# Reordering the first two units' chains of a fused recurrence and expert-mixture kernel

## The chip, the cores and the metric

The kernel runs on one core of a Trainium2 chip. The time is the device time of one execution in microseconds (us). Engines are named as the profile names them: PE is the matrix engine (PEld its weight loads), DVE the vector engine, ACT the scalar engine, POOL the GpSimd engine, and SP the engine that issues nearly all DMA transfers. Each engine works through its own instructions in order and waits on semaphores for the others.

## The reference

The first half is a linear recurrence over 768 time steps for 4 batches and 8 heads with head dimension 40. The second half takes its output as 3072 tokens of 320 numbers and runs four dense two-layer experts over every token, mixed by normalized probabilities.

```
for t in range(S):                      # r,k,v,w,a,b: (4, 8, 768, 40)
    y[:, :, t] = einsum('bhd,bhde->bhe', rt, state)
    Sa = einsum('bhde,bhe->bhd', state, at)
    state = state * wt[:, :, None, :] - einsum('bhd,bhe->bhde', Sa, bt)
    state = state + einsum('bhd,bhe->bhde', vt, kt)
x = y.transpose(0, 2, 1, 3).reshape(3072, 320)
p = domain_probs / (domain_probs.sum(-1, keepdims=True) + 1e-9)
for e in range(4):                      # w1: (4, 320, 1024), w2: (4, 1024, 320)
    out += p[:, e:e+1] * (maximum(x @ w1[e], 0) @ w2[e])
```

## The kernel before

The sequence is cut into 12 chunks of 64 steps, and the batches into two pairs. One pair of batches in one chunk is a *unit*: 24 units, numbered 0 to 23, with units 0 and 1 holding the first chunk. Everything is float32.

For each unit `within(q)`, a generator that the main code advances piece by piece with `run(gen, n)`, computes what needs no state. It transposes the decays `rawW` into `G` and runs a scan for their running products (L413 to L423). PE transposes `G` into `pg`; DVE forms `gp = 1 / (pg * W)` and with it the scaled inputs `n_tok` and `k_tok`, and scales the transposed `AT` by `G`. PE transposes `n_tok` and `k_tok` (`pNT`, `pKT`, copied by ACT into `NT`, `KT`), and multiplies the score matrices `pfe` (which ACT copies to `F`, and DVE masks into `ET`), `pev` (which gives `EV`), and `pc` (the scores of `V` and `R`, masked by DVE into `VC`). For the first three units `V` and `R` are transposed on PE (`pVT`, `pRT`, in `turn_rv`); later units do it on DVE.

`substitute(q, eng)` solves unit-triangular 32x32 systems: it copies `blocks` from `F`, transposes them into `M`, and goes through 16 double columns of `Z`. The first two units do it on DVE, with one product and one reduction for each double column; later units do it on POOL while DVE does other work. `merge(q)` turns the solved `Z` into `Qc` and `QTc`, joins the 32-blocks into 64-blocks on PE (`pY`, `pQ`, both copied by ACT) and fills `QT`. `step(q)` then carries the state: `psat` and `pst`, copies on ACT, `pxr` masked by DVE into `SX`, `pdy` (the output `Y` and the new state, on DVE), and `pxT`, which places `Y` as columns of `xT` for the experts.

The experts follow as pieces of work in a list, taken out by `mix(n)`. In `mixture_of_unit`, used for units 0 and 1, `ups(e)` multiplies `xT` by two pieces of `w1` into `ph` and ACT writes `relu` to `hs`; `down(e)` multiplies `hs` by `w2` into `po`, which DVE scales by the gate and adds to `osb`. `normalize()` forms the gates from the probabilities (`pp` on PE, five small DVE operations). `ph` and `po` share three buffers of PSUM, tagged `mm`; all the other products share five, tagged `big`. Later chunks use a saving scheme of seven products in place of eight.

The order of work around the change is written out by hand, after the definition of `keep_warm`. `keep_warm(n)` issues n products of the identity with itself, whose result nobody reads; each shows as two matrix instructions in the profile. Calls of `load`, `load_raw`, `load_piece` and `load_w2` stand in the same order and go to SP's queue one behind the other. A load into a buffer waits in that queue until the buffer's last reader is done, and all behind it wait too: `rawW` and `rawA` have one buffer each, the `w1` pieces two plus three that borrow `sums`. `tc.keep_in_program_order` (`pin`) fixes an instruction's place on its engine; otherwise a scheduler chooses. From unit 1 on a loop over the units takes over.

Of the kernel before, what the change touches and what calls it, by code (L numbers as in the profile page):

```python
# [15 lines left out]
def kernel(  # L16
# [42 lines left out]
    P = 128  # L59
# [284 lines left out]
    def by(x, n):  # L344
        return x.rearrange("p (h e) -> p h e", e=n)
# [56 lines left out]
    def within(q):  # L402
# [11 lines left out]
        for i in range(2):  # L414
# [1 line left out]
        q.gl = sb.tile([P, 2 * NJ, 1], FP32, name="gl", tag="gl", bufs=4)  # L416
        pin(nc.vector.tensor_tensor(out=q.gl[:], in0=G[:, L::L][:, :, None], in1=first[:, :, 0:1], op=ALU.mult))
        pin(nc.vector.memset(Gv[:, :, 0:1], 0.0))
        pin(nc.vector.tensor_tensor_scan(
            out=G[:, 0:2 * NJ * L], data0=G[:, 0:2 * NJ * L],  # L420
            data1=first[:].rearrange("p c i -> p (c i)"), initial=0.0, op0=ALU.mult, op1=ALU.add,
        ))
        nc.vector.tensor_tensor(out=q.gl[:], in0=q.gl[:], in1=Gv[:, :, L - 1:L], op=ALU.mult)  # L423
        q.AT = sb.tile([P, 2 * NJ, L], FP32, name="AT", tag="AT", bufs=2)
        if q.u == 0:
            pin(turn_raw(q.AT[:], n["rawA"][:]))
        yield

        pg = by(turn("pg", tok(Gv), q.u == 2)[:], 64)[:, :, 0:D]
        gp = sb.tile([P, H, D], FP32, name="gp")  # L430
        pin(nc.vector.tensor_tensor(out=gp[:], in0=pg, in1=n["W"][:], op=ALU.mult))
        pin(nc.vector.reciprocal(out=gp[:], in_=gp[:]))  # L432

        def turn_rv():
            VT = sb.tile([P, 2 * NJ, L], FP32, name="VT", tag="turned", bufs=3)
# [10 lines left out]
            return VT  # L446

        if q.u == 1:
            VT = turn_rv()
        yield  # L450

        def turned(name, x):
# [16 lines left out]
            out=q.N[:, :, 0:D], in0=n["B"][:], scalar=-1.0, in1=gp[:], op0=ALU.mult, op1=ALU.mult,  # L469
        )  # L470
        pin(ins)
        pin(nc.vector.tensor_tensor(out=q.K[:, :, 0:D], in0=n["K"][:], in1=gp[:], op=ALU.mult))
        if q.u > 0:
            pin(turn_raw(q.AT[:], n["rawA"][:]))
        at_ij = q.AT[:].rearrange("p (i j) t -> p i j t", i=2)
        ins = nc.vector.tensor_tensor(out=at_ij, in0=at_ij, in1=Gv.rearrange("p (j i) t -> p i j t", i=2), op=ALU.mult)
        pin(ins)
        q.VC = VCs()
        if q.u > 0:
# [4 lines left out]

        NT = turned("NT", q.N)
        KT = turned("KT", q.K)
        yield

        if q.u > 0:
            if q.u == 2:  # L490
                VT = turn_rv()
            causal_scores(VT)
            yield

# [16 lines left out]
        ))  # L511
        if not q.apart:
            copy_F()
            yield

        ET = ETs()
# [16 lines left out]
            causal_scores(turn_rv())  # L533
        yield

    def substitute(q, eng, between=None):

        blocks = sb.tile([P, H, Q], FP32, name="blocks")
        for i in range(P // Q):
            move = nc.scalar.copy if i >= 2 else nc.vector.tensor_copy  # L540
            tc.keep_in_program_order(move(out=blocks[quarter(i)], in_=q.F[quarter(i), :, quarter(i % 2)]))  # L541
        q.below = belows()
        for i in (1, 3):
            tc.keep_in_program_order(nc.gpsimd.tensor_copy(out=q.below[quarter(i)], in_=q.F[quarter(i), :, 0:Q]))  # L544
# [12 lines left out]
        by_second = Z[:, 1:3].rearrange("p x k r -> p (x k) r")  # L557
        below = M[:].rearrange("p c r -> p (c r)")[:, 1::2 * (Q + 1)]
        ins = nc.vector.tensor_tensor(
            out=by_second, in0=pairs[:, :, 1, :], in1=below[:, :, None].to_broadcast([P, Q // 2, Q]), op=ALU.mult,  # L560
        )
        tc.keep_in_program_order(ins)
        ins = nc.vector.tensor_tensor(out=pairs[:, :, 0, :], in0=pairs[:, :, 0, :], in1=by_second, op=ALU.add)  # L563
        tc.keep_in_program_order(ins)
        run(between)
        at_once = eng is nc.vector
        for x in (0, 3) if at_once else (0,):
            tc.keep_in_program_order(eng.tensor_copy(out=Z[:, x], in_=unit_cols[:]))
        for j in range(0, Q, 2):
            n, m = j // 4 + 1, Q - 1 - j  # L570
            here = 3 * (j // 2 % 2) if at_once else 0
            ins = eng.tensor_tensor(  # L572
                out=Z[:, 1:3, 0:n, j + 1:Q], in0=M[:, j:j + 2, None, j + 1:Q].to_broadcast([P, 2, n, m]),
                in1=Z[:, here, 0:n, j:j + 2].rearrange("p k x -> p x k")[:, :, :, None].to_broadcast([P, 2, n, m]),
                op=ALU.mult,
            )
            if j == 0:
                tc.keep_in_program_order(ins)
            z = Z[:, :, 0:n, j + 1:Q]
            if at_once:  # L580
                terms = z[:, 0:3] if here == 0 else z[:, 1:4]
                eng.tensor_reduce(out=z[:, 3 - here], in_=terms.rearrange("p x k r -> p k r x"), op=ALU.add, axis=AX.X)
            else:
                for x in range(1, 3):
                    eng.tensor_tensor(out=z[:, 0], in0=z[:, 0], in1=z[:, x], op=ALU.add)  # L585
        if at_once:

            odd, even = (Z[:, x].rearrange("p k (r four) -> p k r four", four=4)[:, :, :, 1:3] for x in (3, 0))
            eng.tensor_copy(out=even, in_=odd)
# [405 lines left out]
    def keep_warm(n):  # L995

        for _ in range(n):
            ins = matmul(out=warm[:, 0:P], lhsT=ident[:], rhs=ident[:], start=True, stop=True)
            tc.keep_in_program_order(ins)

    ws = [within(units[u]) for u in range(3)]
    norm = normalize()
    keep_warm(16)
# [10 lines left out]
    go(load_raw(units[2], "W"))  # L1014
    load_probs()
    run(ws[0], 2)

    def scores_of_first():
        run(ws[0], 1)
        yield  # L1020

    substitute(units[0], nc.vector, scores_of_first())
    run(ws[0], 1)
    set_pick()
    m, s = merge(units[0]), begin_step(0)
    run(m, 1)
    run(ws[0])
    load(units[2], "W")
    for x in "VR":
        load_padded(units[2], x)  # L1030
    load_piece()
    load_piece()
    run(ws[1], 1)
    run(norm, 1)
    keep_warm(18)
    run(ws[1], 1)
    run(m)
    run(ws[2], 1)
    run(norm)
    load(units[2], "BK")  # L1040
    go(load_raw(units[2], "A"))
    go(load_raw(begin(3), "W"))
    load_w2(0)
    load_piece()
    load_piece()
    load_w2(1)
    load_piece()
    run(s, 2)
    run(ws[1], 1)
    run(s)  # L1050
    run(ws[1], 2)

    def scores_of_second():
        run(ws[1], 1)
        yield

    mixture_of_unit(units[0])
    substitute(units[1], nc.vector, scores_of_second())
    run(ws[1])
    mix(3)  # L1060
    m, s = merge(units[1]), begin_step(1)
    run(m, 1)
    mix(1)
    run(ws[2], 1)
    run(m)
    run(s, 2)
    run(ws[2], 1)
    load(units[3], "WBKV")
    go(load_raw(units[3], "AVR"))
    mix(1)  # L1070
    run(ws[2], 3)
    substitute(units[2], nc.gpsimd)
    run(ws[2], 1)
    ws.append(within(units[3]))
    run(ws[3], 1)
    mix(1)

    sparse = range(4 * 1, 4 * 4 + 2)

# [124 lines left out]
```

## Time and profile before

| | |
|---|---|
| median of 3 runs | 1113.57 us (1108.56 to 1113.94) |
| the profiled execution | 1112.43 us, its span 1110.2 us, mean granted PE clock 0.988 |
| busy: PE, PEld | 1075.2 us (97%), 959.7 us (86%) |
| busy: DVE, POOL, ACT | 758.1 us (68%), 501.5 us (45%), 352.9 us (32%) |
| moved by DMA | 122.18 MB, 110 GB/s on average |

Busy times are those of one profiled execution, counted from the start of its span. A timeline row gives the start, the busy time, the engine and line, the operation, what it writes and reads, how many instructions were joined in the row, and in brackets the idle time of the engine just before with what ended it. A row of the windows gives, for a stretch of time, its length, the busy time of PE, PEld, DVE, ACT and POOL (with counts), the PE clock granted (1.00 is full speed), the DMA engines' busy share and the GB/s moved. PE is busy for nearly all of the span, and its gaps lie in the first 160 us.

### The profile page before, as it was taken

How to read it: one execution, taken by the hardware profiler on the slowest of the kernel's cores; microseconds unless marked ns; L12 is line 12 of the kernel's file. 1: busy time of each engine (PE TensorE's matmuls, PEld its weight loads, DVE VectorE, ACT ScalarE, POOL GpSimd, SP SyncE). 2: the span in 40 equal slices, each digit the busy share in tenths (PEclk: the TensorE clock that was granted, in tenths of full speed). 3: DMA queues.
4: the chain of work that ended last, by engine and by line, in shares of the span. 5: the costliest groups of instructions: out<-in, count | busy, mean ns of one | idle time of the engine just before them, and what ended most of it. 6: DMA issues, size and time to landing. Idle time of an engine off the chain costs nothing.

```text
span 1110.2 us, 38530 instructions
## 1 busy us (share of the span) xinstructions
PE 1075.2 (97%) x16100; PEld 959.7 (86%) x16100; DVE 758.1 (68%) x1553; ACT 352.9 (32%) x956; POOL 501.5 (45%) x1272
## 2 busy tenths in 40 slices
PE   6799899999999999999999999999999999999998
PEld 5677788788898998989989899998989989988887
DVE  8765578888777767768667677767677677543443
ACT  2323434333333233232342333332432332322110
POOL 5004576781643734634635636536437346330000
PEclk8899999999999999999999999999999999999999
DMA  7785535444354364454443453543553532222320
GB/s 120 207 249 139 115 77 127 112 98 113 96 135 94 93 156 101 104 123 112 103 120 89 121 120 93 125 104 98 132 109 80 145 88 65 90 77 70 101 87 12
DMA packets 268868, 122.18 MB, mean 110 GB/s; under 512 B 213736, under 2 KB 242072, under 8 KB 268696
## 3 DMA queue, kind: packets, MB, share of 16 engines
q1 hardware_dynamic: 265416, 119.12, 43.6%
q8 instruction: 127, 2.08, 0.8%
q10 hardware_dynamic: 3280, 0.61, 0.3%
q14 instruction: 45, 0.37, 0.1%
HBM read 111.79 MB, written 3.93 MB: 104 GB/s over the span
## 4 chain that ended last, share of the span: by engine, by line
PE 77%; DVE 4%; POOL 3%; ACT 2%; issue 2%; SPq 2%; DMA 1%; DVEq 0%; POOLq 0%
PE ph L76 34%; PE p L76 27%; PE pdy L76 2%; POOL Z L585 2%; PE psat L76 2%; PE pxr L76 2%; PE prn L76 1%; PE po L76 1%; PE pfe L76 1%; POOL Z L572 1%; PE pQ L76 1%; PE pc L76 1%; PE pev L76 1%; PE pe L76 1%; PE pY L76 1%
## 5 line engine op out<-in xcount | busy, mean ns | idle before, releaser
L76 PE MATMUL ph<-xT,w1p 128*128 128x256 f32 (+3 forms) x3040 | 445.1, 376 | 1.9 <-issue 1.7
L76 PEld LDWEIGHTS ph<-xT,w1p 64*64 64x64 f32 (+1 forms) x3040 | 337.5, 161 | 70.2 <-issue 26.9
L585 POOL TENSOR_TENSOR Z<-Z 128x31 f32<-128x31 f32 (+7 forms) x704 | 256.7, 365 | 55.1
L889 DVE TENSOR_TENSOR a<-hs 128x512 f32<-128x512 f32 x220 | 151.3, 705 | 106.3 <-ACT hs L770 106.1
L572 POOL TENSOR_TENSOR Z<-M,Z 128x62 f32<-128x62 f32 (+7 forms) x352 | 148.5, 422 | 130.1 <-DVE M L563 104.2
L770 ACT ACTIVATE hs<-ph 128x512 f32<-128x512 f32 (+1 forms) x208 | 115.1, 564 | 229.0 <-PE ph L76 227.8
L76 PE MATMUL p<-sums,a 128*128 128x160 f32 x1056 | 164.9, 299 | 0.0
L76 PEld LDWEIGHTS p<-sums,a 128*128 128x128 f32 x1056 | 152.8, 190 | 2.2
L783 DVE SCALAR_TENSOR_TENSOR osb<-p,gate,osb 128x320 f32<-128x320 f32 (+1 forms) x243 | 108.1, 481 | 57.7 <-PE p L76 53.5
L544 POOL COPY below<-F 32x256 f32<-32x256 f32 x48 | 23.0, 480 | 219.8 <-ACT F L502 218.2
L76 PE MATMUL p<-w,a 128*128 128x160 f32 x704 | 106.2, 301 | 0.8 <-ACT hs L770 0.6
L76 PE MATMUL p<-w,hs 128*128 128x160 f32 x704 | 102.9, 299 | 0.0
L76 PEld LDWEIGHTS p<-w,hs 128*128 128x128 f32 x704 | 100.2, 190 | 2.2
L76 PEld LDWEIGHTS p<-w,a 128*128 128x128 f32 x704 | 98.3, 190 | 3.9 <-ACT hs L770 3.9
L604 POOL COPY QT<-QTc 32x256 f32<-32x256 f32 x96 | 50.2, 523 | 75.8 <-DVE QTc L598 38.6
L547 DVE STREAM_TRANSPOSE M<-blocks 128x1024 f32<-128x1024 f32 x24 | 47.3, 1972 | 38.3 <-ACT blocks L541 38.2
L692 ACT COPY RS<-pxr 64x256 f32<-64x256 f32 x88 | 32.3, 367 | 108.7 <-DVE SX L400 60.0
L432 DVE RECIPROCAL gp<-gp 128x320 f32<-128x320 f32 x24 | 51.6, 2151 | 0.7
L529 ACT COPY EV<-pev 64x160 f32<-64x160 f32 x96 | 23.1, 286 | 89.3 <-PE pev L76 89.0
L619 ACT COPY QT<-pQ 32x128 f32<-32x128 f32 x96 | 24.6, 257 | 59.4 <-PE pQ L76 57.7
L596 DVE STREAM_TRANSPOSE Qc<-Z 128x256 f32<-128x256 f32 x24 | 15.1, 628 | 39.9 <-POOL Z L585 39.8
L651 ACT COPY SN<-prn 128x256 f32<-128x256 f32 x44 | 14.9, 372 | 78.5 <-DVE RH L646 77.4
(147 smaller groups left out, 1369.2 us busy)
## 6 DMA issues: line engine op xcount, KB each, us to landing
w1p<-in_moe_w_dram SPq DMA_DIRECT2D x95, 512.0 KB
w1p<-in_moe_w_dram SPq DMA_DIRECT2D x190, 64.0 KB
w<-in_moe_w_dram SPq DMA_DIRECT2D x4, 1280.0 KB
sums<-in_moe_w_dram SPq DMA_DIRECT2D x9, 512.0 KB
natW<-in_w_dram SPq DMA_DIRECT2D x48, 80.0 KB
natB<-in_b_dram SPq DMA_DIRECT2D x48, 80.0 KB
natK<-in_k_dram SPq DMA_DIRECT2D x48, 80.0 KB
out_dram<-osb SPq DMA_DIRECT2D x46, 80.0 KB
```

Of the source, the lines that this page charges most:

```text
L76: return stated(nc.tensor.matmul(**k))
L432: pin(nc.vector.reciprocal(out=gp[:], in_=gp[:]))
L529: nc.scalar.copy(out=of_slot(q.EV[half(p)], i ^ p)[:, :, 0:D], in_=pev[i][half(p)])
L547: ins = nc.vector.transpose(out=M[:], in_=cols)
L572: ins = eng.tensor_tensor(out=Z[:, 1:3, 0:n, j + 1:Q], in0=M[:, j:j + 2, None, j + 1:Q].to_broadcast([P, 2, n, m]), in1=Z[:, here, 0:n, j: ...
L585: eng.tensor_tensor(out=z[:, 0], in0=z[:, 0], in1=z[:, x], op=ALU.add)
L604: ins = nc.gpsimd.tensor_copy(out=q.QT[quarter(i), :, quarter(i % 2)], in_=QTc[quarter(i)])
L619: nc.scalar.copy(out=of_slot(to[quarter(2 * r)], y), in_=src)
L692: nc.scalar.copy(out=RS[half(s), x ^ s::2], in_=prs[x][half(s)].rearrange("p (j i) t -> p j i t", i=2),)
L770: nc.scalar.activation(out=h[:, i * HF // 2:(i + 1) * HF // 2, 0:n], in_=ph[i][:], func=ACTF.Relu,)
L783: nc.vector.scalar_tensor_tensor(out=to, in0=p, scalar=sc, in1=to, op0=ALU.mult, op1=ALU.add)
L889: nc.vector.tensor_tensor(out=t[:], in0=x, in1=y, op=op)
```

## The change

The change is in the generator `within` and in the order written out by hand; no product of the computation is added or taken away.

- **Spare products.** The 18 directly ahead of the first merge go. 12 are put behind unit 0's `pe`, 4 behind its `pc`, 3 ahead of the merge.
- **Unit 1's chain.** Its scan moves behind unit 0's solve on DVE (the transposes of `G` stay ahead of it). `turn_rv` is called at a yield of its own. `pg` moves behind `pQ` of the merge, `pNT` and `pKT` behind `pdy`; its `k_tok` and its scaling of `AT` go from DVE to POOL.
- **Unit 1's solve** begins behind unit 0's `Y`. It has a new argument `during`, which issues other work between its columns: the gates of `normalize` and the first `down`.
- **Unit 2's chain.** `G` and its scan go behind unit 1's merge transposes on DVE; `V` and `R` are turned right behind `KT`; `pc` goes behind `pfe`, and `ET` ahead of `blocks`.
- **Loads.** On SP's queue `w2` of the first expert and the pieces behind it stand ahead of unit 2's `B` and `K`. Unit 3's `rawW` goes from ahead of all these to behind `w2` of the third expert, ahead of pieces 7 and 8. Pieces 9 and 10 of `w1` stand ahead of unit 3's `W`, `B`, `K`, `V`, `A` and `R`.
- **PE's order** is fixed to program order from the start and not only from the loop on.

From `pdy` of unit 1 on, the instructions of PE stand in the same order in both kernels.

```diff
@@ within(q)
         pin(nc.vector.memset(Gv[:, :, 0:1], 0.0))
-        pin(nc.vector.tensor_tensor_scan(...))
-        nc.vector.tensor_tensor(out=q.gl[:], in0=q.gl[:], in1=Gv[:, :, L - 1:L], op=ALU.mult)
         q.AT = sb.tile([P, 2 * NJ, L], FP32, name="AT", tag="AT", bufs=2)
-        if q.u == 0:
-            pin(turn_raw(q.AT[:], n["rawA"][:]))
-        yield
...
         if q.u == 1:
+            yield
             VT = turn_rv()
+            yield
+        pin(nc.vector.tensor_tensor_scan(
...
+        if q.u < 2:
+            pin(turn_raw(q.AT[:], n["rawA"][:]))
+        yield
+
+        pg = by(turn("pg", tok(Gv), q.u == 2)[:], 64)[:, :, 0:D]
...
-        pin(nc.vector.tensor_tensor(out=q.K[:, :, 0:D], in0=n["K"][:], in1=gp[:], op=ALU.mult))
-        if q.u > 0:
+        other = nc.gpsimd if q.u == 1 else nc.vector
+        pin(other.tensor_tensor(out=q.K[:, :, 0:D], in0=n["K"][:], in1=gp[:], op=ALU.mult))
+        if q.u > 1:
             pin(turn_raw(q.AT[:], n["rawA"][:]))
...
-        ins = nc.vector.tensor_tensor(out=at_ij, in0=at_ij, ...)
+        ins = other.tensor_tensor(out=at_ij, in0=at_ij, ...)
...
         KT = turned("KT", q.K)
-        yield
-
-        if q.u > 0:
-            if q.u == 2:
-                VT = turn_rv()
+        if q.u == 2:
+            VT = turn_rv()
+        yield
+
+        if q.u == 1 or q.u >= PADDED:
             causal_scores(VT)
             yield
...
         if not q.apart:
             copy_F()
+            if q.u == 2:
+                causal_scores(VT)
             yield
@@ substitute
-    def substitute(q, eng, between=None):
+    def substitute(q, eng, between=None, during=None):
...
         for j in range(0, Q, 2):
+            if during:
+                during(j)
@@ the order by hand
+    in_order[0] = True
     ws = [within(units[u]) for u in range(3)]
...
     load_probs()
     run(ws[0], 2)
-    def scores_of_first():
+    keep_warm(12)
+    def scores_of(u):
...
-    substitute(units[0], nc.vector, scores_of_first())
+    substitute(units[0], nc.vector, scores_of(0))
     run(ws[0], 1)
     set_pick()
     m, s = merge(units[0]), begin_step(0)
     run(m, 1)
     run(ws[0])
+    keep_warm(4)
+    run(norm, 1)
+    run(ws[1], 1)
+    keep_warm(3)
     load(units[2], "W")
     for x in "VR":
         load_padded(units[2], x)
     load_piece()
     load_piece()
     run(ws[1], 1)
-    run(norm, 1)
-    keep_warm(18)
-    run(ws[1], 1)
-    run(m)
-    run(ws[2], 1)
-    run(norm)
-    load(units[2], "BK")
     go(load_raw(units[2], "A"))
-    go(load_raw(begin(3), "W"))
     load_w2(0)
     load_piece()
     load_piece()
+    run(m)
+    run(ws[1], 1)
+    run(s, 3)
+    run(ws[1], 1)
+    run(s, 1)
+    run(ws[1], 1)
+    run(s)
+    load(units[2], "BK")
     load_w2(1)
     load_piece()
-    run(s, 2)
-    run(ws[1], 1)
-    run(s)
     run(ws[1], 2)
...
     mixture_of_unit(units[0])
-    substitute(units[1], nc.vector, scores_of_second())
-    run(ws[1])
-    mix(3)
+    def during_second(j):
+        if j in (0, 14):
+            mix(1)
+        if j == 4:
+            run(ws[1])
+        if j == 12:
+            run(norm)
+    substitute(units[1], nc.vector, scores_of(1), during_second)
     m, s = merge(units[1]), begin_step(1)
     run(m, 1)
+    run(ws[2], 1)
+    go(load_raw(begin(3), "W"))
+    mix(2)
+    run(ws[2], 1)
+    run(m, 1)
+    lead()
+    run(m)
     mix(1)
     run(ws[2], 1)
-    run(m)
     run(s, 2)
     run(ws[2], 1)
     load(units[3], "WBKV")
     go(load_raw(units[3], "AVR"))
+    run(ws[2], 2)
+    substitute(units[2], nc.gpsimd)
     mix(1)
-    run(ws[2], 3)
-    substitute(units[2], nc.gpsimd)
-    run(ws[2], 1)
     ws.append(within(units[3]))
     run(ws[3], 1)
-    mix(1)
```

More of the change, by code (lines that the diff above doesn't have):

```diff
@@ L418, in within @@
         pin(nc.vector.memset(Gv[:, :, 0:1], 0.0))
[L419 to L422, printed above, removed]
-        nc.vector.tensor_tensor(out=q.gl[:], in0=q.gl[:], in1=Gv[:, :, L - 1:L], op=ALU.mult)
-        q.AT = sb.tile([P, 2 * NJ, L], FP32, name="AT", tag="AT", bufs=2)
-        if q.u == 0:
-            pin(turn_raw(q.AT[:], n["rawA"][:]))
-        yield
[L429 to L432, printed above, removed]
+        q.AT = sb.tile([P, 2 * NJ, L], FP32, name="AT", tag="AT", bufs=2)
         def turn_rv():
@@ L448, in within @@
         if q.u == 1:
+            yield
             VT = turn_rv()
+            yield
+        pin(nc.vector.tensor_tensor_scan(
+            out=G[:, 0:2 * NJ * L], data0=G[:, 0:2 * NJ * L],
+            data1=first[:].rearrange("p c i -> p (c i)"), initial=0.0, op0=ALU.mult, op1=ALU.add,
+        ))
+        nc.vector.tensor_tensor(out=q.gl[:], in0=q.gl[:], in1=Gv[:, :, L - 1:L], op=ALU.mult)
+        if q.u < 2:
+            pin(turn_raw(q.AT[:], n["rawA"][:]))
+        yield
+        pg = by(turn("pg", tok(Gv), q.u == 2)[:], 64)[:, :, 0:D]
+        gp = sb.tile([P, H, D], FP32, name="gp")
+        pin(nc.vector.tensor_tensor(out=gp[:], in0=pg, in1=n["W"][:], op=ALU.mult))
+        pin(nc.vector.reciprocal(out=gp[:], in_=gp[:]))
         yield
@@ L471, in within @@
         pin(ins)
-        pin(nc.vector.tensor_tensor(out=q.K[:, :, 0:D], in0=n["K"][:], in1=gp[:], op=ALU.mult))
-        if q.u > 0:
+        other = nc.gpsimd if q.u == 1 else nc.vector
+        pin(other.tensor_tensor(out=q.K[:, :, 0:D], in0=n["K"][:], in1=gp[:], op=ALU.mult))
+        if q.u > 1:
             pin(turn_raw(q.AT[:], n["rawA"][:]))
         at_ij = q.AT[:].rearrange("p (i j) t -> p i j t", i=2)
-        ins = nc.vector.tensor_tensor(out=at_ij, in0=at_ij, in1=Gv.rearrange("p (j i) t -> p i j t", i=2), op=ALU.mult)
+        ins = other.tensor_tensor(out=at_ij, in0=at_ij, in1=Gv.rearrange("p (j i) t -> p i j t", i=2), op=ALU.mult)
         pin(ins)
@@ L1016 @@
     run(ws[0], 2)
-    def scores_of_first():
-        run(ws[0], 1)
+    keep_warm(12)
+    def scores_of(u):
+        run(ws[u], 1)
         yield
-    substitute(units[0], nc.vector, scores_of_first())
+    substitute(units[0], nc.vector, scores_of(0))
     run(ws[0], 1)
@@ L1045 @@
     load_piece()
+    run(m)
[6 more added lines that the diff above has]
+    load(units[2], "BK")
     load_w2(1)
     load_piece()
-    run(s, 2)
-    run(ws[1], 1)
-    run(s)
     run(ws[1], 2)
-    def scores_of_second():
-        run(ws[1], 1)
-        yield
     mixture_of_unit(units[0])
-    substitute(units[1], nc.vector, scores_of_second())
-    run(ws[1])
-    mix(3)
+    def during_second(j):
[6 more added lines that the diff above has]
+    substitute(units[1], nc.vector, scores_of(1), during_second)
     m, s = merge(units[1]), begin_step(1)
     run(m, 1)
+    run(ws[2], 1)
[5 more added lines that the diff above has]
+    run(m)
     mix(1)
     run(ws[2], 1)
-    run(m)
     run(s, 2)
```

## The prediction

> **What bounds the kernel now.** I read the page's slices first, then PE's waits behind 170 us, then PE's timeline up to there, then DVE's in the gaps, and last the windows for the clock.
>
> ```profile
> PE   6799899999999999999999999999999999999998
> ...
> PE ph L76 <- issue: 1.7, 2, 1.3
> PE pc L76 <- DVE RT L241: 0.9, 1, 0.9
> PE p L76 <- ACT hs L770: 0.6, 2, 0.3
> PE pxr L76 <- issue: 0.5, 1, 0.5
> PE pxr L76 <- ACT SX L672: 0.4, 1, 0.4
> ```
>
> The slices: PE is at 90% or more except in the first five. The waits (total us, times, longest) are those of 170 us to the end: 4.1 us in 940. PE's order from unit 1's `pdy` (103.96 us) on is unchanged. So the change is worth what it takes off PE's arrival there: a gain in the head is kept one to one, and nothing else can be gained.
>
> PE's timeline, in the head:
>
> ```profile
> 20.79 1.32 PE L76 MATMUL pev<-VC,ET 64*64 64x40 f32 x32 [5.97 <-DVE ET L400]
> ...
> 32.51 6.26 PE L76 MATMUL warm<-ident 128*128 128x128 f32 x36
> 38.70 0.68 PE L76 MATMUL pY<-QTc,below 64*64 64x64 f32 x16
> ...
> 51.70 2.60 PE L76 MATMUL ph<-xT,w1p 64*64 64x128 f32 x32
> ...
> 68.47 2.75 PE L76 MATMUL ph<-xT,sums 64*64 64x128 f32 x32 [1.80 <-DVE osb L781]
> ...
> 96.40 0.94 PE L76 MATMUL pev<-VC,ET 64*64 64x40 f32 x29 [2.00 <-DVE ET L400]
> ...
> 97.82 6.21 PE L76 MATMUL ph<-xT,sums 128*128 128x128 f32 x48
> ...
> 114.79 0.84 PE L76 MATMUL pc<-RT,VT 40*64 40x64 f32 x32 [1.92 <-DVE RT L241]
> ```
>
> And what DVE had done meanwhile:
>
> ```profile
> 32.66 0.45 DVE L598 STREAM_TRANSPOSE QTc<-Qc 128x256 f32<-128x256 f32 x1
> ```
>
> `QTc` was there at 33.1 us, but `pY`, which needs it, stood behind 36 spare instructions until 38.70. Those also did something, as the windows show (PEclk is the third figure from the end):
>
> ```profile
> 30.00:32.00 2.00, 0.78 (x5) 0.38 (x3) 1.76 (x10) 1.11 (x3) 0.00 (x0) 0.50 0.99 308
> 34.00:36.00 2.00, 2.00 (x11) 2.00 (x11) 1.97 (x2) 0.00 (x0) 0.80 (x3) 0.50 0.00 0
> 36.00:38.00 2.00, 2.00 (x17) 2.00 (x16) 1.93 (x5) 0.00 (x0) 0.00 (x0) 0.83 0.00 0
> 38.00:40.00 2.00, 1.38 (x23) 1.12 (x22) 1.82 (x6) 0.50 (x2) 0.00 (x0) 1.00 0.59 87
> 98.00:100.00 2.00, 2.00 (x11) 2.00 (x12) 1.86 (x4) 0.71 (x3) 1.76 (x4) 0.53 0.83 291
> 100.00:102.00 2.00, 2.00 (x24) 1.60 (x22) 0.00 (x0) 0.45 (x2) 1.64 (x5) 0.62 0.19 56
> ```
>
> The clock was at half from about 20 us and came back near 36.6 us, inside the spare products. It halved again at 98 us, after the 2.00 us wait for `ET`.
>
> **The change part by part.** I rebuild PE's times with durations from the timelines; all are of the profiled execution (span 1110.2, time 1112.43, which is 1.1 below the median).
>
> *First solve.* Unit 1's scan and `gl` (1.23 + 0.2 us) leave DVE ahead of it. `blocks` started at 16.00, held by them; `F` was copied at 15.03. So `blocks` starts at 15.05; ACT's half of it ends at 15.87, and `M`, before at 16.79, starts at 16.0. `QTc` comes at 32.3: 0.8 earlier. The 12 spare products behind `pe` (24 instructions at the 0.12 us of the ones at 8.72) end at 17.7, before `pev` at 20.0: free. The 4 behind `pc`, then `pp`, `pVT`, `pRT` and the last 3 take at half clock 1.4 + 0.7 + 1.1 + 1.0 + 1.0 us from 25.6, ending by 30.8: free too, as `QTc` comes at 32.3.
>
> *Merge and first step.* `pY` at 32.35. From `pY` to `psat` took 2.98 (41.68 less 38.70), to the end of `pst` 4.9; `pg` (0.6) now stands between but half of it fits the wait for ACT's `QT`: `pst` ends at 37.4. `pNT` and `pKT` (1.05) no longer stand ahead of `pxr`, which starts at 37.5 and ends at 38.2. DVE meanwhile: masks of `VC` to 33.1, scan, `gl`, transpose of `AT` (2.1) to 35.2, then, behind `pg`, `gp` and its reciprocal (0.47 + 2.15) to 38.2. `SX` waits there behind the reciprocal, by nothing. From `SX` to the end of `pdy` took 2.53 (45.34 to 47.87): 40.7. `pNT`, `pKT` 1.05: 41.8; from `pxT` to `ph` 2.96: `ph` starts at 44.75 in place of 51.70. That is **-6.95** at full clock. The cover is thin at one place: `n_tok` (0.49, after `SX`) is ready at 39.5, `pNT` wants it at 40.7.
>
> *POOL.* No row shows a product that size there. POOL's products took 0.29 for 62 elements and 0.46 for 152, so 0.8 and 1.15 by that slope for 320 and 512; behind the reciprocal they end at 39.0 and 40.2, and `pKT` and `pfe` want them at 41.2 and 43.8. Behind them in POOL's queue is only `below`. [...] The trace: `k_tok` on DVE took 0.68 beside POOL's solve (111.06) and 0.48 without it (79.14), so 0.2. [...]
>
> *Clock.* This is the unknown that counts. [...] But in the row above a gap of 2.00 us was enough for about 3.4 us of half clock. I go by the row. At half clock `pVT` took 1.11 against 0.60, `pc` 1.69 against 0.69; if it holds from 33 us for two such stretches, `pQ`, `pg`, `psat` with `pst` and `pxr` lose about 0.5, 0.5, 1.2 and 0.7: **+3**. Bounds: 0, and +6 if `pdy`, `pNT`, `pKT` and `pxT` run at half as well; from there PE has no gaps, which brought the clock back both times.
>
> *Unit 1's solve to `po` of the second expert.* It starts 7 earlier with `ph`. The gates (1.2 us in all) now lie inside it; `osb` stands earlier among its columns, about 58.5, and `po` ends before. The 1.80 wait of `ph` for `osb` (its PSUM buffer) falls to some 0.3: **-1.5**. `pg` of unit 2 now waits for its `G`: DVE has `QTc` at 64.4, `G` and scan to 67.0, `po` ends at 66.1: **+0.95**. The 1.25 us "issue" gap at 54.66 has no cause in the trace; I let it stay (bounds: 0 and -1.25).
>
> *Unit 2.* `pfe` is ahead of `pc`, which waits for ACT's `RT` 0.8 in place of 0.62: **+0.2**. `ET` comes ahead of `blocks` on DVE, at about 82.7, and `pev` behind `po` and a piece of `ph` at 86.2: the wait of 2.00 goes, **-2.0**, and with it the half clock (48 `ph` in 6.21, where 46 took 4.41 at 80.66): **-1.7**. POOL's third solve starts after `M`, 9 earlier, ends near 107.6, and `pY` wants it near 111.
>
> *SP's queue.* `rawA`, first in it now, waits for the transpose of `AT` at 35.2; before, `natB` waited until 36.9. `w2` of the first expert goes out at 37.3 (before 43.73), wanted near 52. `rawW` of unit 3 waits for unit 2's `G` at 65.5, and pieces 7 and 8 and the last `w2` behind it go out from 67.5 to 74 (before 66.7 to 73.4), wanted from 88. Pieces 9 and 10 wait for 4 and 5 (read until 76.3), then unit 3's loads (16.3 us of issuing) end at 94.3, land near 96, and DVE wants `rawR` near 102. **0**, with 5 us to spare. The wait for `RT` ahead of unit 3's `pc` (1.92) stays: its DVE chain starts from `pdy` as before.
>
> Sum: -6.95 + 3 - 1.5 + 0.95 + 0.2 - 2.0 - 1.7 = **-8.0**. The profiled span would be 1102.2, its time 1104.4; against the median, 1105.5.
>
> **The rivals.** *The clock holds* through the merge: without the +3, -11, 1102.5. For it: 7 us of unbroken PE work from 24 us on, which should end the half clock by 30. Against: the gap behind it, and the 2.00 us row.
> *The clock stays low* up to the first `ph`, the +6 bound: -5, 1108.5.
> *The gain is lost to other waits*, a new "issue" gap and thrice 2 us for `pg`, `pc` and `osb`: about 1113. Against: PE's waits in the trace all have a DVE or ACT cause that moves along.
> *SP's queue becomes the bound*, slower: its stream stands no earlier at 94 us than before (94.3 against 94.15) while PE is 8 to 11 earlier. [...] Every us by which `rawR` lands later than 102 is a us of PE idle. It decides from 6 us late on; to end slower than before it must be 14 late, to be seen as slower 20 (about 1120). Against: SP waited 28.5 us for `ph` up to 200 us, so it has room.
>
> **How the numbers follow.** Likeliest case 0.46, clock holds 0.22, clock low 0.18, lost 0.07, SP bound 0.07. About 0.5% (5.6 us) is what can be told from no change: faster is below 1108.0, slower above 1119.1. The likeliest case gives 0.40 of faster (half clock and "issue" gap move it by 3, the runs spread by 5.4), clock holds 0.21, clock low 0.07: 0.68. Slower is SP alone and a little spread: 0.07. The rest 0.25. The range reaches from the clock held with the "issue" gap gone (1101.2), less some 4 of the spread of 5.4 (1097), to the lost case with a little spread (1114).
>
> **What would show it.** Right: `pY` near 32.4, first `ph` near 45 to 48, no wait of `pev` for `ET` at unit 2, unit 1's `pdy` near 93 to 96 and everything behind it shifted by that. The clock step is read from the windows of 32 to 44 us. Wrong: a wait ahead of `ph` or `po` on a DMA, `pc` of unit 3 waiting over 3 us for `RT`, or a shift of `pdy` that is not found again at the end.

## The result, and the profile after

| | before | after |
|---|---|---|
| median | 1113.76 us (1108.56 to 1115.11) | 1102.41 us (1100.13 to 1104.31) |
| ratio, 95% interval | | 0.9903 (0.988 to 0.9926) |
| profiled execution: time, span | 1112.43, 1110.2 us | 1102.3, 1100.6 us |
| PE busy, mean granted clock | 1075.2 us, 0.988 | 1070.0 us, 0.991 |

The change makes the kernel about 1% faster, 11.35 us by the medians and 9.6 us by the spans of the two profiled executions. The prediction was 1105.5 us, from 1097 to 1114. The sum came out near, in part by luck: two of its terms were wrong and made up for each other, and some 1.8 us that it did not have were won and given back later.

The page's slices of the changed kernel:

```profile
PE   6799899999999999999999999999999999999998
```

And PE's waits from 170 us to the end (total us, times, longest):

```profile
PE ph L76 <- issue: 2.6, 2, 2.1
PE pc L76 <- DVE RT L241: 0.9, 1, 0.9
PE pxr L76 <- ACT SX L680: 0.4, 1, 0.4
PE p L76 <- ACT hs L778: 0.2, 1, 0.2
```

As before, PE is full behind the first slices, and waits 4.1 us in all behind 170 us. So the head is where the time went, but one wait there has grown: `ph` on "issue", 2.1 us at the longest in place of 1.3. It comes back below.

PE's timeline in the head:

```profile
20.30 0.91 PE L76 MATMUL pev<-VC,ET 64*64 64x40 f32 x32 [2.30 <-DVE ET L400]
...
32.98 1.11 PE L79 MATMUL pRT<-ident,padded 128*128 128x128 f32 x4 [3.83 <-DVE VC L400]
33.88 1.49 PE L76 MATMUL warm<-ident 128*128 128x128 f32 x6
35.30 1.05 PE L76 MATMUL pY<-QTc,below 64*64 64x64 f32 x16
...
37.58 0.68 PE L76 MATMUL pQ<-Yq,Qc 64*64 64x64 f32 x14 [0.22 <-ACT Yq L627]
38.19 0.66 PE L79 MATMUL pg<-ident,G 128*128 128x128 f32 x4
...
48.55 2.60 PE L76 MATMUL ph<-xT,w1p 64*64 64x128 f32 x32
...
69.75 0.66 PE L79 MATMUL pg<-ident,G 128*128 128x128 f32 x4 [0.47 <-DVE G L439]
...
88.67 0.62 PE L76 MATMUL pev<-VC,ET 64*64 64x40 f32 x32
...
89.71 4.63 PE L76 MATMUL ph<-xT,sums 128*128 128x128 f32 x48
...
104.97 0.69 PE L76 MATMUL pc<-RT,VT 40*64 40x64 f32 x32 [1.78 <-DVE RT L241]
```

`pY` starts at 35.30 us, 3.40 earlier than before but 2.95 later than predicted. In front of it stands a wait that the prediction did not have: `pRT` of unit 1 waited 3.83 us for DVE's mask of `VC`. Unit 2's `pev` no longer waits for `ET`, and the 48 `ph` behind it take 4.63 us in place of 6.21, at full clock.

DVE at the place of the new wait:

```profile
32.15 0.45 DVE L606 STREAM_TRANSPOSE QTc<-Qc 128x256 f32<-128x256 f32 x1
32.52 0.74 DVE L400 COPY_PREDICATED VC<-mask_up,pc 128x256 f32<-128x256 int32 x2
```

The masks of `VC` are the last readers of unit 0's `pc`, and they come behind `QTc`. `pRT` needed one of the two PSUM buffers that `pc` held (the kernel gives `pc` two of the five `big` ones). So `pY`, whose input was there at 32.6, stood behind `pRT` and three spare products.

The windows of the changed kernel (PE's busy time is the second figure, its clock the third from the end, the DMA engines' share the last but one):

```profile
34.00:36.00 2.00, 2.00 (x20) 1.78 (x20) 1.45 (x3) 1.10 (x3) 1.15 (x2) 0.50 0.21 72
36.00:38.00 2.00, 1.09 (x23) 0.82 (x22) 0.00 (x0) 1.02 (x4) 0.00 (x0) 0.96 0.45 92
...
40.00:42.00 2.00, 2.00 (x80) 2.00 (x74) 1.56 (x1) 1.43 (x5) 0.30 (x1) 0.50 1.02 353
42.00:44.00 2.00, 1.55 (x52) 1.26 (x49) 1.75 (x3) 0.36 (x2) 1.79 (x2) 0.76 1.07 397
...
98.00:100.00 2.00, 2.00 (x9) 1.38 (x8) 1.97 (x3) 0.00 (x0) 1.69 (x5) 1.00 0.32 63
```

The clock was at half until about 36, back at full until 39.5, and at half again until 43. The stretch at 98 us, at 0.53 before, is at full clock.

PE's starts in the two profiled executions, against the steps of the sum. Each row is the time from the last event to this one, after less before:

| stretch of PE's order | predicted | measured | from the starts, before and after |
|---|---|---|---|
| to `pY` of unit 0 | -6.35 | -3.40 | 38.70, 35.30 |
| `pY` to first `ph` | -0.60, clock +3 | +0.25 | 51.70, 48.55 |
| first `ph` to the first `po` | 0 | -1.21 | 59.61, 55.25 |
| to the second `po` (wait for `osb`) | -1.5 | -1.87 | 71.05, 64.82 |
| to `pg` of unit 2 | +0.95 | +0.62 | 75.36, 69.75 |
| to `pev` of unit 2 | -1.8 | -2.12 | 96.40, 88.67 |
| to `pdy` of unit 1 | -1.7 | -1.95 | 103.96, 94.28 |
| **all to `pdy` of unit 1** | **-8.0** | **-9.68** | |
| to `pY` of unit 2 (past unit 3's `pc`) | 0 | -1.73 | 122.98, 111.57 |
| from there to the end | 0 | +1.81 | spans 1110.2, 1100.6 |

### The profile page after: what moved, and what is told of

Its sections match the earlier page's. It is cut to its first block, busy times and chain, and to the rows that moved or that the text cites. A ratio compares the mean times of both kernels' runs of the same rounds, so it can differ in the third digit from the quotient of the medians.

```text
span 1100.6 us, 38528 instructions
## 1 busy us (share of the span) xinstructions
PE 1070.0 (97%) x16102; PEld 955.8 (87%) x16102; DVE 756.6 (69%) x1551; ACT 353.0 (32%) x956; POOL 502.9 (46%) x1274
## 3 DMA queue, kind: packets, MB, share of 16 engines
q8 instruction: 127, 2.08, 0.8%
## 4 chain that ended last, share of the span: by engine, by line
PE 81%; DVE 7%; POOL 5%; ACT 3%; issue 2%; DMA 1%; SPq 0%; ACTq 0%; DVEq 0%; POOLq 0%
PE ph L76 35%; PE p L76 28%; POOL Z L593 3%; PE pdy L76 3%; PE psat L76 2%; PE pxr L76 2%; POOL Z L580 2%; PE prn L76 1%; PE pfe L76 1%; PE pQ L76 1%; PE po L76 1%; PE pc L76 1%; DVE Z L590 1%; PE pY L76 1%; DVE M L553 1%
## 5 line engine op out<-in xcount | busy, mean ns | idle before, releaser
L593 POOL TENSOR_TENSOR Z<-Z 128x31 f32<-128x31 f32 (+7 forms) x704 | 260.0, 369 | 55.2
L580 POOL TENSOR_TENSOR Z<-M,Z 128x62 f32<-128x62 f32 (+7 forms) x352 | 144.1, 409 | 132.3 <-DVE M L569 106.4
```

Source lines behind the costliest of these rows:

```text
L580: ins = eng.tensor_tensor(out=Z[:, 1:3, 0:n, j + 1:Q], in0=M[:, j:j + 2, None, j + 1:Q].to_broadcast([P, 2, n, m]), in1=Z[:, here, 0:n, j: ...
```

## The experiments

The theory was: the gain is PE's earlier arrival, made at `pY`, at `osb`, and at unit 2's `ET`; what it fell short by at `pY` is the PSUM buffer; and the clock in the merge is worth a few microseconds. The rivals: that taking the spare products away is the whole gain, that the clock is worth nothing, and that waits elsewhere take what the buffer would give. A single pair of profiles places a gain; a difference at the end under about 4 us is within what the runs of one kernel spread (4.2 us in six runs of the changed kernel). No run tries the moved gates, the new order of the loads or PE's fixed order alone; what is said of `osb` below is read from the two profiles.

**The removal alone.** The kernel before without its 18 spare products, and nothing else changed.

```diff
-    keep_warm(18)
```

> The kernel before, with only the 18 spare products ahead of the first merge taken out. All theories: pY follows QTc at about 33.2 us instead of 38.7. Mine: without them the clock stays at half through the merge (it came back inside them), so that of the 5.5 us some 3 are given back before the first ph (near 49 us), and the end comes 2.5 us earlier than in the kernel before. Rival, spare products only stood in the way: the whole 5.5 us is kept. Rival, they are worth what they cost: no gain or a loss.

Measured: 1108.23 us (1107.54 to 1110.59), ratio to before 0.9958 (0.9945 to 0.9972). PE's timeline of this kernel:

```profile
33.33 1.12 PE L76 MATMUL pY<-QTc,below 64*64 64x64 f32 x16 [2.96 <-DVE QTc L598]
```

`pY` came 5.37 us earlier, waiting for `QTc` alone, but the clock stayed at half until 42 us, so the first `ph` came at 49.02, only 2.68 earlier: 15.69 us from `pY` to `ph` in place of 13.00. In the profile 4.9 us are left at the end, more than at `ph`; here, for one thing, the half clock behind unit 3's `pc` did not come (the windows from 112 to 116 us are at 1.00). So by the medians the removal is under half of the change's gain, and the spare products did earn some 2.7 us of what they cost.

**The buffer.** The changed kernel with the spare products' tile in the PSUM buffers of `ph` and `po`, which are idle then.

```diff
-    warm = big("warm")
+    warm = ps.tile([P, 512], FP32, name="warm", tag="mm", bufs=3)
```

> The changed kernel, with the PSUM tile of the spare products taken from the three mm buffers, which nobody uses before the first ph, instead of one of the five big ones. Mine: pRT of unit 1 waited 3.8 us because the five big buffers were taken (two by pc until DVE's VC mask behind QTc), and pY stood behind it; with a buffer free, pRT ends before 31 us, pY starts at 32.7 in place of 35.3, and 2 to 3 us are gained at the first ph and at the end (1100). Rival, the wait has another cause or is replaced (DVE's reciprocal, the clock falling in the gap ahead of pY): below 1 us or nothing.

Measured: 1101.73 us (1100.57 to 1102.71), ratio 0.9902 (0.9874 to 0.9929). PE's timeline:

```profile
28.97 1.06 PE L79 MATMUL pRT<-ident,padded 128*128 128x128 f32 x4
29.82 1.49 PE L76 MATMUL warm<-ident 128*128 128x128 f32 x6
33.09 0.68 PE L76 MATMUL pY<-QTc,below 64*64 64x64 f32 x16 [1.77 <-DVE VC L400]
```

The 3.83 us wait of `pRT` is gone, so the buffer was its cause. Now `pY` itself waits for the same mask of `VC`, as the next buffer in turn is one of `pc`'s two; that is why it starts at 33.09 and not at 32.6, when `QTc` is there. It starts 2.21 earlier than in the changed kernel, and the first `ph` at 45.92 is 2.63 earlier: inside the 45 to 48 us that the prediction named, where the changed kernel's 48.55 is not. Of the 2.63, 1.8 are left at the end of its profile; the medians differ by 0.68, which these runs do not tell from nothing.

**The other spare products.** The changed kernel without the groups of 12, 4 and 3.

```diff
-    keep_warm(12)
...
-    keep_warm(4)
...
-    keep_warm(3)
```

> The changed kernel without its 19 new spare products (12, 4 and 3). Mine: pY starts some 1.5 us earlier, behind pRT alone (near 33.9), but the clock is at half from about 20 us through the whole merge, psat, pxr, pdy and pxT, which costs 3 to 5 us: first ph 1.5 to 3.5 us later than in the changed kernel (50 to 52), the end as much later. Rival, spare products at these places are idle decoration: the 1.5 us is gained (first ph near 47).

Measured: 1105.69 us (1100.97 to 1110.43), ratio 0.9935 (0.9913 to 0.9958). PE's timeline:

```profile
33.05 1.12 PE L76 MATMUL pY<-QTc,below 64*64 64x64 f32 x16 [4.59 <-DVE VC L400]
34.83 1.67 PE L76 MATMUL pQ<-Yq,Qc 64*64 64x64 f32 x16 [0.67 <-ACT Yq L627]
36.43 1.11 PE L79 MATMUL pg<-ident,G 128*128 128x128 f32 x4
```

`pY` starts where it did in the kernel with the other buffer, since the spare tile's buffer now comes free early too; the expectation, which had it behind `pRT`, was wrong in that. So the two can be set side by side: the same start of `pY` (33.05 and 33.09), but the first `ph` at 49.13 and 45.92. `pQ` takes 1.67 us and `pg` 1.11 at half clock, which lasted from 18 to 45 us; with the other buffer it came back at 31.7 and was at half again only from 35.2 to 38.6. From `pY` to `ph` that makes 16.08 us against 12.83. Of the 3.25 between them 0.41 is an "issue" gap ahead of `pfe` (below), so the clock is worth about 2.8, and that is what the spare products earn. At the end nothing is decided: this profile is the slowest of ten runs, which lie between 1100.97 and 1110.43.

**Unit 2's `ET`.** The changed kernel with `pfe`'s mask back behind the preparation of unit 2's solve on DVE.

```diff
-    run(ws[2], 2)
+    run(ws[2], 1)
     substitute(units[2], nc.gpsimd)
     mix(1)
+    run(ws[2], 1)
```

> The changed kernel with unit 2's ET mask put back behind the preparation of its solve on DVE, as it stood in the kernel before; nothing else. Mine: pev of unit 2 waits again, for ET near 90 us, 1.5 us, and the clock may fall to half behind that wait, another 0 to 1.7: unit 1's pdy and the end 1.5 to 3.2 us later. Rival, the wait for ET is covered by what comes behind it (POOL's solve, the wait of unit 3's pc for RT): no difference at the end.

Measured: 1105.16 us (1102.31 to 1106.22), ratio 0.993 (0.9909 to 0.9951). PE's timeline:

```profile
89.27 0.94 PE L76 MATMUL pev<-VC,ET 64*64 64x40 f32 x29 [1.08 <-DVE ET L400]
```

The wait for `ET` is back with 1.08 us, and from the first `ph` to unit 1's `pdy` PE takes 47.33 us in place of 45.73: 1.6 of the 3.7 that the prediction gave to this step. Not all of the 1.6 is `ET`'s: the "issue" gap inside `pfe` is 0.99 here and was 0.47, though part of that is covered by a shorter wait for `RT` behind it (0.17 for 0.42). No half clock follows; the 48 `ph` take 4.63 here too. So the wait is what the place of `ET` decides, and whether half clock follows it is another matter.

**POOL's two products.** The changed kernel with unit 1's `k_tok` and scaling of `AT` back on DVE.

```diff
-        other = nc.gpsimd if q.u == 1 else nc.vector
+        other = nc.vector
```

> The changed kernel with unit 1's k_tok and its scaling of AT given back to DVE; nothing else. Mine: on POOL they blocked DVE's n_tok (1.22 us beside them, 0.49 alone), so DVE gains little from giving them away. Back on DVE, n_tok takes 0.5, k_tok and AT follow by 44.6 us, just before Y is wanted at 44.8: first ph within 0.5 us of the changed kernel's 48.55, the end within 1. Rival, the move to POOL is worth the 1.2 us that DVE is freed of: Y and the first ph come 1.2 us later, and so does the end.

Measured: 1103.34 us (1101.93 to 1107.74), ratio 0.9917 (0.9891 to 0.9944): no difference to the changed kernel. DVE's timeline in the changed kernel:

```profile
42.92 1.22 DVE L471 SCALAR_TENSOR_TENSOR n_tok<-natB,gp 128x320 f32<-128x320 f32 x1
44.76 0.76 DVE L715 TENSOR_TENSOR Y<-pdy,G 128x256 f32<-128x256 f32 x2 [0.62 <-PE pdy L76]
```

POOL's beside it:

```profile
41.70 0.86 POOL L476 TENSOR_TENSOR k_tok<-natK,gp 128x320 f32<-128x320 f32 x1 [6.50 <-issue]
42.52 1.27 POOL L480 TENSOR_TENSOR AT<-AT,G 128x512 f32<-128x512 f32 x1
```

And DVE's in this kernel:

```profile
43.04 0.48 DVE L471 SCALAR_TENSOR_TENSOR n_tok<-natB,gp 128x320 f32<-128x320 f32 x1
43.44 0.49 DVE L476 TENSOR_TENSOR k_tok<-natK,gp 128x320 f32<-128x320 f32 x1
43.84 0.69 DVE L480 TENSOR_TENSOR AT<-AT,G 128x512 f32<-128x512 f32 x1
44.88 0.76 DVE L715 TENSOR_TENSOR Y<-pdy,G 128x256 f32<-128x256 f32 x2 [0.35 <-PE pdy L76]
```

Beside POOL's product of 512 elements `n_tok` took 1.22 us, alone 0.48. With POOL left out DVE does all three products in 1.5 us, and `Y` starts at 44.88 in place of 44.76. Both ways it waits for `pdy`, so neither costs anything.

**More spare products in the free stretch.** The other buffer, and the group ahead of the merge at 7 in place of 3.

```diff
-    warm = big("warm")
+    warm = ps.tile([P, 512], FP32, name="warm", tag="mm", bufs=3)
...
-    keep_warm(3)
+    keep_warm(7)
```

> The changed kernel with the spare products' tile in an mm buffer and with 7 of them, in place of 3, ahead of the merge. Mine: PE is then busy until about 33 us, when pY can start, the clock stays at full in the merge, where it fell back to half from 35.5 to 38.7 us with 3 of them: pQ, pg and psat take 1 to 1.5 us less, the first ph comes near 44.8 (45.9 with 3, 48.55 in the changed kernel), the end 3 to 4 us earlier than the changed kernel (ratio to the kernel before near 0.987). Rival, the four more only delay pY (the windows of the clock lie as they lie): first ph at 46 to 47, no gain over 3 of them. Rival, what is won in the head is lost behind it in issue gaps: first ph early, but the end not more than 1 us earlier than the changed kernel.

Measured: 1101.18 us (1098.69 to 1102.93), ratio 0.9892 (0.9867 to 0.9917). It is the fastest of all here by its median; the changed kernel, on the same chip, gave 1104.45, and their intervals overlap. PE's timeline:

```profile
32.80 0.68 PE L76 MATMUL pY<-QTc,below 64*64 64x64 f32 x16 [0.43 <-DVE VC L400]
...
50.07 0.72 PE L76 MATMUL ph<-xT,w1p 128*128 128x128 f32 x5 [2.52 <-issue]
```

`ph` first came at 45.51, 3.04 earlier than in the changed kernel. Then PE stood for 2.52 us on "issue" at 50.07 and for 2.28 at 125.26; in the changed kernel the first of these is missing and the second is 1.32. So at `ph` the first expectation was near, and in this execution the third, that gaps elsewhere take the gain, came true. But this execution is the slowest of five (1098.69 to 1102.93). By the medians 3.27 us are left against the changed kernel on the same chip, which is what the first expectation gave for the end; the intervals overlap, so the runs do not decide between the two.

**The changed kernel once more**, to see what moves by itself.

> The changed kernel as it is, beside the two others, for a second profile. If the clock's falls lie at fixed places of the program, the half clock is found again at 22 to 36 and 39.5 to 43 us; if they depend on where a free-running window falls, the places move by up to 3 us while the waits stay, and the first ph by about 1 us (48.55 and 47.9 have been seen with the same head).

Measured: 1104.45 us (1102.81 to 1105.92), ratio 0.9921 (0.9899 to 0.9943). By kind, the waits up to 130 us are those of the first profile to within 0.3 us. The clock is not. The windows of this profile:

```profile
38.00:40.00 2.00, 2.00 (x52) 1.57 (x49) 0.99 (x2) 1.03 (x4) 0.00 (x0) 1.00 0.81 162
40.00:42.00 2.00, 1.68 (x77) 1.35 (x69) 2.00 (x3) 1.69 (x6) 0.20 (x1) 1.00 1.05 389
```

Half clock ended near 36.5 as before, and the second fall, from 39.5 to 43 us, did not come. With that the first `ph` came at 48.37.

The two profiles show one thing more, and those of four other kernels agree with it. Inside the span a stretch of half clock lasts 3.41 us or a whole multiple of that: 13.65 (22.49 to 36.14) and 3.41 (39.55 to 42.97) in the first profile, 13.65 (22.92 to 36.57) in this one, 17.07, 3.41 and 3.41 in the kernel before; by the windows 3.41 (35.15 to 38.56) with the other buffer, 3.40 (103.56 to 106.96) with 7 spare products, and 27.3, eight times 3.41, without 19 spare products (17.7 to 45.0). In the kernel before and in the two profiles of the changed one all changes of the clock lie on a grid with steps of 3.41 us, and the grid lies differently in each: 2.55 us past a multiple of the step before, 2.01 in the first profile, 2.44 in this one.

**What the "issue" gaps are.** The two gaps of the fastest version are 3.5 us more than the changed kernel has at those places, as much as it had won at `ph`; and one had left the changed kernel (the 1.25 us at 54.66, which the prediction let stay). I counted PE's matrix instructions from the start of the span up to each such gap (a few records can be missing, so the count is good to 1 or 2). In the kernels told so far the gaps of 0.4 us and more up to 200 us, but for one of 0.39 that two kernels have ahead of `psat`, stand in front of these numbers:

| number | kernels (gap in us, ahead of) |
|---|---|
| 470 | without 19 spare products (0.41, `pfe`) |
| 596 to 597 | before (1.25, `ph`), other buffer (1.70, `ph`), 7 spare products (2.52, `ph`), `ET` late (0.64, `ph`) |
| 974 to 975 | after (0.47, `pfe`), other buffer (0.84, `pfe`), `ET` late (0.99, `pfe`), no POOL (0.46, `pfe`), without 19 (1.20, `pc`) |
| 1735 to 1736 | after (1.32, `ph`), again (1.05), other buffer (1.32), no POOL (2.31), 7 spare products (2.28), `ET` late (0.52) |
| 2875 to 2877 | before (0.55, `pxr`), without 18 (1.24, `ph`), without 19 (1.68, `ph`) |

The numbers stay where they are while up to 38 instructions ahead of them come or go. They lie 127, 3 x 127, 6 x 127 and 9 x 127 apart, to within 4. And the page has a queue of which nothing was said so far (packets, MB, share):

```profile
q8 instruction: 127, 2.08, 0.8%
```

PE issued 16102 matrix products; over 127 packets that is 126.8 each. So the reading is: PE's instructions themselves come in these packets, about 127 products to each, and the gap is a packet that came late. The trace has the times of that queue's packets. The one for number 1735 of the changed kernel starts at 123.10 and takes 1.12 us, so it landed at 124.22; the gap began at 124.30 and ended at 125.62, 1.41 behind the landing. Each of the 19 gaps in the table ended 1.2 to 1.6 us behind the landing of such a packet. Two kernels were made to test the reading, both the changed kernel with nothing but the number of spare products at the start altered: 18 matrix instructions more, and 56 fewer.

```diff
-    keep_warm(16)
+    keep_warm(20)
...
-    keep_warm(10)
+    keep_warm(15)
```

> The changed kernel with 4 and 5 more spare products in the two groups ahead of unit 0's first products: 18 more matrix instructions in PE's stream, nothing else. It asks what the gaps called issue belong to. In the kernels so far such gaps stand in front of PE's matrix instruction number 597, 974 or 975, 1735 or 1736, 2242 and 2875 to 2877, counted from the start, whatever is computed there: 127 or a multiple of it apart, and 16102 instructions over the page's 127 packets of its instruction queue are 126.8. Theory one, the instructions themselves come late in pieces of 127: if a gap of over 0.5 us stands near 120 to 127 us, it stands again in front of number 1735 or 1736, which is now an operation 18 earlier in the program. Theory two, the gap belongs to the operation (ph of the experts, which waits for something that the profile does not name): it stands in front of number 1753. The other gap, number 3188 at 209.6 us, has moved with the operation in all kernels so far: expected at 3206 by both. Time within 2 us of the changed kernel.

```diff
-    keep_warm(16)
+    keep_warm(6)
...
-    keep_warm(10)
+    keep_warm(4)
...
-    keep_warm(12)
```

> The changed kernel with 28 spare products fewer ahead of and behind unit 0's first products (groups of 6, 4 and 0 in place of 16, 10 and 12): 56 matrix instructions fewer in PE's stream; the clock will be lower in the first 20 us, which is not the question. Number 1735 is now an operation 56 later, which comes near 129 us, inside ph, where the DMA engines are busy 0.2 to 0.4 of the time, in place of behind a stretch at 1.07. Theory one, instructions come late where the DMA engines were full: no gap over 0.5 us at number 1735, and none in front of number 1679 either, which is the operation that had it. Theory two, the gap belongs to the operation: again 1 to 2 us in front of number 1679. Number 597 falls 56 operations later too, in a stretch at 1.05: by theory one a gap of 0.5 to 2.5 us may come there, at number 597. The gap of the operation that was number 3188: at 3132 by both.

Measured, one run each: 1108.26 and 1108.88 us. PE's timeline, first with 18 more, then with 56 fewer:

```profile
128.75 0.50 PE L76 MATMUL pxr<-RT,SN 64*64 64x64 f32 x9 [3.06 <-issue]
```

```profile
128.27 0.69 PE L76 MATMUL pxr<-RT,SaT 64*64 64x64 f32 x30 [1.20 <-issue]
```

With 18 more the gap stands again in front of number 1735, now in the middle of `pxr` and not ahead of `ph`; the other gaps are at 470, 2877 and 3512, which is 5 x 127 further. With 56 fewer neither 1735 nor 1679 has a gap, and one of 1.20 us stands in front of number 1608, 127 less than 1735; 470 has one of 0.76, 3765 one of 1.02, and 597 has none. The gap does not belong to the operation; it belongs to the place in the stream. All seven gaps named here, too, ended 1.3 to 1.5 us behind a packet's landing. With 18 more the packet for number 1735 started at 126.14, when PE had already stood for 0.45 us. The expectation of the time was not met by the first: 18 spare instructions that were to be nearly free came out 6 us slower in the one run made, with 0.90 and 3.06 us of such gaps, half clock from near 127 us on at the second, and a first `ph` 2.08 later.

The gap of the changed kernel at 209.56 is of another kind. It stood in front of number 3188, 3196 with the 8 more instructions, 3150 without the spare products, 3206 and 3132 in the last two: it moves with its operation, the third product of a group of `ph` with 64 rows, behind two that have run. The last packet had landed 4.9 us before it ended. Though the rows say "issue", the trace shows what it waits for: an instruction of PE that does nothing but wait for semaphores ended at 209.50, and the one that came last is DVE's. PE's and DVE's timelines, first before and then after:

```profile
220.31 4.74 PE L76 MATMUL ph<-xT,w1p 64*64 64x256 f32 x30 [1.30 <-issue]
219.81 0.40 DVE L783 SCALAR_TENSOR_TENSOR osb<-p,minus_gate,osb 128x160 f32<-128x160 f32 x1
```

```profile
209.56 6.38 PE L76 MATMUL ph<-xT,w1p 64*64 64x256 f32 x30 [2.09 <-issue]
209.09 0.37 DVE L791 SCALAR_TENSOR_TENSOR osb<-p,minus_gate,osb 128x160 f32<-128x160 f32 x1
```

In all eleven profiles this gap ends 0.10 us behind the end of that DVE instruction. It reads a `p`, which shares the three `mm` buffers with `ph`, so by the kernel's text it is once more a buffer's last reader. PE came to its two first products 11.53 us earlier than before (206.83 and 218.36), DVE to this instruction only 10.72, and so the gap grew by 0.8.

In the windows of the changed kernel:

```profile
208.00:210.00 2.00, 0.44 (x8) 0.41 (x11) 2.00 (x5) 0.00 (x0) 0.00 (x0) 1.00 0.49 96
210.00:212.00 2.00, 2.00 (x15) 1.13 (x7) 2.00 (x5) 0.00 (x0) 1.60 (x3) 0.56 0.72 124
```

Before, the gap was 1.30 and the same 30 products took 4.74 us, at full clock; now it is 2.09, the clock falls behind it, and they take 6.38. That is 0.79 and 1.64 us, 2.4 together. Unit 4's `pdy` was still 11.54 earlier than before (189.59 and 201.13); a `pc` behind the gap is 9.11 earlier (246.33 and 255.44). So the 1.81 that went on the way to the end went here.

## Why the prediction was right, and where it was not

*What bounds the kernel.* Right: PE's order behind unit 1's `pdy` was worth what PE arrived earlier, -9.68 there and -9.6 at the end. The "kept one to one" was so only on balance, and by luck: 1.73 more came at unit 3's `pc`, and 1.81 went again, 2.4 being lost at 209.56, where PE waits for DVE.

*First solve and `pY` at 32.35.* The step that failed. `QTc` came only 0.5 us earlier and not 0.8, which is small. But the prediction said that the four spare products, `pp`, `pVT`, `pRT` and the last three "end by 30.8: free too". It had added up their durations and not asked where their results go: five PSUM buffers, one of them held by the spare products' tile and two by `pc`, whose last reader stands behind `QTc` on DVE. With `pp` and `pVT` in the last two, `pRT` waited 3.83 us, and `pY` came 2.95 late. The kernel with the other buffer shows the cause, and what it costs: 2.21 us at `pY` and 2.63 at the first `ph`. Even there `pY` started 0.74 later than forecast, some 0.25 for `QTc` and the rest for the mask.

*Clock, +3.* Right in kind, too large. The clock was at half in the merge, but from `pY` to `ph` PE took 13.25 us where the prediction had 12.4 at full clock: 0.85. The half clock lay elsewhere than the prediction put it: over `pY` (1.05 us for 0.68) and again from 39.55 us over the end of `psat`, `pst` and `pxr`, but not over `pQ` and `pg`, which took 0.68 and 0.66, as at full clock. The upper bound of +6 was not reached either: with half clock up to 45 us, and an "issue" gap of 0.41, `pY` to `ph` took 16.08 us, 3.7 over 12.4. These two errors, +2.95 - 2.15, left the first `ph` 0.80 later than forecast.

*The row of 2.00 us.* The prediction let a gap of 2.00 us bring half clock, as the kernel before had it at 98 us. The changed kernel itself doesn't decide it, as its gap became 3.83. The kernel with the other buffer comes nearer: its longest gap there was 1.77 us, and the clock, at full from 31.74 us on, was at half again from 35.15 to 38.56. So half clock came there without a gap of 2.00. But the row misled too: a gap of 1.78 us ahead of unit 3's `pc` was followed by half clock with 7 spare products and not in the changed kernel, and one of 2.52 us by none. The grid of 3.41 us lay differently in the two profiles of the changed kernel, and with the same waits the clock fell a second time in the one and not in the other. The grid also sorts most of the gaps. Those of 2.28, 2.31 and 2.52 us that brought no half clock were each cut by it, into parts of 1.06 and 1.22, 1.25 and 1.06, 1.40 and 1.12; of the two of 2.00 (before) and 2.09 us that did bring it, 1.69 and all of the 2.09 lay in one step. It does not sort those near 1.8: one of 1.78 whole in a step brought half clock with 7 spare products and none in the changed kernel's second profile. A threshold can't be read from these runs. Half clock followed some of the gaps, and the stretch behind each of those named in this paragraph was one step of 3.41 us.

*`osb`, `pg` and unit 2.* Right within 0.4 us each: -1.87, +0.62, -2.12 and -1.95 against -1.5, +0.95, -1.8 and -1.7. With `ET` put back late, 1.6 of the last two came back.

*The "issue" gap of 1.25 us, left to stay.* Wrong; its lower bound came true. It went, less a new wait of 0.58 for `ET`. It had a cause in the trace: before, the packet for instruction number 597 landed at 54.43, and the gap ended 1.48 later; in the changed kernel it landed at 49.46, before PE had come there. The DMA engines were at 0.83 and 0.64 around that packet (46 to 48 and 48 to 50 us) and at 1.05 to 1.08 around the other; that this made it early is likely, but not shown. Number 1735 has a new gap of 1.32 us, which ended 1.41 behind a packet's landing at 124.22.

*Unit 3's `pc`, forecast to stay as it is.* The wait for `RT` did stay (1.78 for 1.92), but the half clock behind it did not come: 32 `ph` took 2.60 us in place of 4.09. It is the clock again (the grid cuts this gap into 1.22 and 0.56), and not the change by itself: the kernel before without 18 spare products has no half clock there either.

*POOL's two products.* The sum has no term for them, and the run with both back on DVE shows none: `Y` starts at 44.88 in place of 44.76 and waits for `pdy` both ways. The slack alone is the reason. The estimates of 0.8 and 1.15 us came out as 0.86 and 1.27. That DVE would lose 0.2 beside them was wrong: `n_tok` lost 0.7 (1.22 us beside POOL's product of 512 elements, 0.48 with POOL left out). The 0.2 was read from a row beside smaller products of POOL.

*SP's queue.* It did not become the bound: unit 3's `rawR` was issued from 95.27 to 99.79 us, some 5 later than worked out, and PE's wait at `pc` is for DVE's chain.

*The rivals.* "Lost to other waits" was right in kind and small: new "issue" gaps of 0.47 and 1.32 us, and 1.8 us in all from `pY` of unit 2 to the end. The clock held through the whole merge in no run; nearest were the second profile of the changed kernel and the one with `ET` late, where half clock ended at 36.6 and 36.9, just behind `pY`, and did not come back there. SP's queue did not matter.

## What to carry to other kernels

Adding up the durations of a moved group of products shows that they fit; it must also be asked whose buffer each result takes, and when that buffer's last reader is done: here that was a wait of 3.83 us. In this kernel, which one engine bounds, a gap there had its length as a price, and behind some gaps half clock as a second one (2.09 us at 209.56, and 6.38 in place of 4.74 for the 30 products behind it). The filler products were worth some 2.8 us; they are worth keeping where they take nothing from a path and hold no buffer. Before a gap without a releaser is explained by its operation, count the instructions ahead of it in two kernels. Where the number stayed here, as 1735 did with 18 instructions more, the gap belonged to the instruction stream, and the edit ahead moved what it hit, from `ph` to `pxr`. Where it moved with the operation, as from 3188 to 3206, an instruction of another engine ended just ahead of the gap's end in every profile, by 0.10 us: look for that one.

## What was not expected of the hardware

- PE stands for 0.4 to 3.06 us at fixed numbers in its instruction stream, 127 matrix products or multiples of that apart. Each such gap ended 1.2 to 1.6 us behind the landing of a packet of the instruction queue. Ahead of many the DMA engines were at about full share: 1.05 to 1.08 before the 1.25 us gap, 1.22 before that of 2.52, 1.05 before that of 3.06. But full queues are not needed: ahead of the 1.02 us gap at number 3765 they were at 0.09 to 0.10 from 248 to 254 us; there PE had gone through the 127 products before it in 2.9 us. Why a packet is late is thus open; no run changed the DMA traffic alone. A gap comes only at some of the packets: in the changed kernel two landed at 56.91 and 85.50 us with none behind them.
- The clock changes on a grid of 3.41 us in these profiles (stretches of half clock of 3.41, 13.65 and 17.07 us), and half clock does not follow the length of a single gap. Gaps of 1.77 and 1.78 us were followed by half clock in two kernels, gaps of 2.28, 2.31 and 2.52 us by none, and those of 2.09 and 3.06 us by it.
- The kernel with 18 spare instructions more came out some 6 us slower in its one run, with 2.6 us more of "issue" gaps in front of two numbers alone. Differences of a few microseconds between kernels with different numbers of instructions are not to be put down to the edit unless the stretch that it touches shows them.
